# Hashed attention and a PReLU layer pair on one core: the last store's buffer and queue, the place of the maxima and the verdict, and the pair of x's first differences

## The chip, the cores and the metric

The kernel runs on one core of a Trainium2 chip. The metric is the device time of one execution in microseconds (us), the median of several runs. One more execution of the kernel was recorded by the hardware profiler; all rows below come from that recording. The engines are PE (TensorE: matmuls and transposes through the array), DVE (VectorE), ACT (ScalarE), POOL (GpSimd) and SP (SyncE, which here only issues DMAs). ACT and POOL issue DMAs too.

## What is computed

```python
# q, k, v: (4, 8, 768, 64) f32, proj: (64, 6)
q_bucket = sum over 6 bits of (q @ proj > 0) * 2**bit      # k_bucket likewise
scores = where(q_bucket == k_bucket, q @ k.T / 8, -1e9)    # per batch and head
x = softmax(scores) @ v  ->  (3072, 512)                   # heads beside each other
h = x @ w_in                                               # (3072, 2048)
g = max(h, 0) + alpha * min(h, 0)
out = g @ w_out                                            # (3072, 512) f32
```

## The kernel before, in words

There are two paths. `fast_path` computes the result; while it runs it also takes the largest magnitudes of the inputs (`largest`, lines 1079 to 1083), and `verdict` (lines 1085 to 1097) turns them into one flag. After `fast_path` PE, ACT, DVE and SP each load the flag (line 401) and branch (line 402): the general path is only entered if the flag says that the fast one wasn't safe, which is not so on these inputs. So the end of the program is, on each of these engines: its last instruction, the load of the flag, the branch over the general path, and the closing waits and barriers (lines 402 and 1284). SP's closing waits are one per DMA completion semaphore.

The fast path has two stages.

**Attention** (line 1134): 16 iterations `pi`, one for a pair of heads. PE computes scores (`sc`, line 734), ACT takes their exponentials into `pt` (line 737), DVE sums these (`accp` and `accd`, lines 745 to 759), PE multiplies with v (`av`, line 770) and adds the sums up over partitions (`sm`, line 784), and DVE divides (`divide`, line 789) in the next iteration. Beside this DVE rounds pieces of the weights (lines 587 to 644) and, in the last pairs, forms differences of x of the first batch (`sum_x`, line 842: one subtraction of 128x768 a call, read by `load_x` from DRAM, line 832).

**Products** (line 1202): 4 batches `b`. Each has 8 blocks of the first product (`f_0` to `f_7`) and 7 of the second (`z_1, z_2, z_5, z_6, z_3, z_7, z_4`), 60 blocks in all, counted by `j` in the loop. Every block is a 2x2 product done with 7 matrix products in place of 8 (steps 1, 2, 5, 6, 3, 7, 4 of `Product.step`) with sums kept in three PSUM banks a, b, c; DVE and ACT form the sums and differences around it (lines 877, 915, 919, 923, 979, 987, 1008). The engines' orders are written out by hand: each `do(...)` keeps its place in program order on its engine, so a late instruction holds all that is behind it. In the first batch alone DVE also sums up the pieces of w_out (`sum_out`, line 963).

In the before kernel `largest` runs at `j == 4` (block f_4 of batch 0) and `verdict` at the end of the same block: four small DVE instructions, a PE transpose of 128x4 (`vd`, line 1087, into bank b), and nine more on DVE.

**The end.** Blocks of z are stored as they finish. `turn_out` transposes on DVE and issues 12 stores of 32 KB on SP (line 1040). The last two parts go through `turn_last`: for the last but one, six PE transposes, two ACT copies into `o` and one store of 384 KB on ACT's queue (line 1062). For the last, PE transposes into three PSUM places `tx`, `ty`, `tz`; ACT copies `ty` into `o2`, which is stored on ACT's queue (line 1070); DVE copies `tx` (line 1068) and `tz` (line 1071) into `o`, which is stored on SP's queue (line 1072). All these `o` share the tag `o`, which has two buffers.

In the built program, every DMA that SP or ACT issues adds to one of eight completion semaphores, which are handed out in turn over both queues, in the order in which the DMAs stand in the program. A DMA's issue waits, where needed, for the one before it on the same semaphore. The 12 stores of line 1040 that belong to block z_3 and the last three stores stand in this order before the change, with the number of their semaphore: six of line 1040 (7, 0, 1, 2, 3, 4), line 1062 (5), two of line 1040 (6, 7), line 1070 (0), four of line 1040 (1, 2, 3, 4), line 1072 (5). After the change: six of line 1040 (7, 0, 1, 2, 3, 4), line 1062 (5), two of line 1040 (6, 7), line 1070 (0), one of line 1040 (1), line 1072 (2), three of line 1040 (3, 4, 5).

Of the kernel before, what the change touches and what calls it, by code (L numbers as in the profile page):

```python
# [8 lines left out]
F32 = mybir.dt.float32  # L9
# [397 lines left out]
def fast_path(  # L407
# [12 lines left out]
    nc = tc.nc  # L420
    P = 128
# [21 lines left out]
    PE, DVE, ACT, POOL = nc.tensor, nc.vector, nc.scalar, nc.gpsimd  # L443
# [117 lines left out]
    def load_weight(i):  # L561
        if i < NW:
            i = order[i]
            raw[i] = pool.tile([P, 512], moe_w_in.dtype, name=f"raw{i}", tag="raw", bufs=3)
            nc.sync.dma_start(raw[i], piece(i))
# [17 lines left out]
    def weight_clamp(i):  # L583
        if i < NW:
            i = order[i]
            x = wx[i]
            do(DVE.tensor_scalar(x, x, HI_MIN, None, op0=ALU.max, op1=ALU.max, accum_out=wmax[:, i : i + 1]))

    def weight_parts(i):
        i = order[i]  # L590
        lo, hi = halves(i)
        x = wx[i]
        wr[i] = r = pool.tile([P, 512], F32, name=f"wr{i}", tag="wr", bufs=1)
        do(DVE.tensor_scalar(
            x.bitcast(U32), x.bitcast(U32), 3, 0xC0000000, op0=ALU.logical_shift_left, op1=ALU.bitwise_xor,
        ))
        do(DVE.tensor_scalar(r.bitcast(U32), x.bitcast(U32), 0x7F800000, None, op0=ALU.bitwise_and))
        do(DVE.scalar_tensor_tensor(r, lo, 2.0 ** -52, r, op0=ALU.mult, op1=ALU.mult))
# [65 lines left out]
    def two_banks(name):  # L664
        return psum.tile([P, 2, 512], F32, name=name, tag="sc", bufs=3)
# [77 lines left out]
    def add_first(pi):  # L743
        accp[pi] = pool.tile([P, 2 * NCH, CW], F32, name=f"accp{pi}", tag="accp", bufs=1)
        do(DVE.tensor_tensor(accp[pi], p(0), p(1), op=ALU.add))  # L745
        if pi:
            nc.gpsimd.dma_start(accp[pi][:, 2:], p(2)[:, 2:], accum_op=ALU.add)
# [6 lines left out]
    def add_third(pi):  # L754
        n = 2 if pi else 4
        do(DVE.tensor_tensor(accp[pi][:, :n], accp[pi][:, :n], p(2)[:, :n], op=ALU.add))
# [66 lines left out]
    def pinned(when, ins):  # L823

        if when:
            do(ins)

    def load_x(b, *ns):
        for n in ns or range(4):
            m, kh, ch = ((0, 0, 0), (1, 1, 0), (2, 1, 1), (5, 0, 1))[n]  # L830
            t = mid.tile([P, 2, CW], F32, name=f"x{b}_{m}", tag=f"x{m}", bufs=1)
            pinned(b == 0, nc.sync.dma_start(
                t, x_s[b, 2 * kh : 2 * kh + 2].rearrange("k p s -> p k s")[:, :, ch * CW : (ch + 1) * CW],
            ))
            x_m[b, m] = t

    def sum_x(b, n, engine):

        to, a, c = ((3, 5, 0), (5, 2, 5), (4, 2, 3), (6, 4, 1))[n]
        if to != 5:  # L840
            x_m[b, to] = mid.tile([P, 2, CW], F32, name=f"x{b}_{to}", tag=f"x{to}", bufs=1)
        do(engine.tensor_tensor(x_m[b, to], x_m[b, a], x_m[b, c], op=ALU.subtract))
# [202 lines left out]
    def turn_last(n):  # L1045


        b, p, half, ch = to_turn.pop(0)
        dst = out_v[b, ch * CH : (ch + 1) * CH].rearrange("c p d -> p c d")[:, :, half * 2 * P : (half + 1) * 2 * P]

        def cells(name, at):
            ps = two_banks(f"{name}{p}")[:, 0].rearrange("p (t f) -> p t f", f=P)
            for k, (t, i) in enumerate(at):
                do(PE.transpose(ps[:, k], m2[b, p][:, i, t * P : (t + 1) * P], ident))
            return ps[:, : len(at)]

        if n == 0:
            o = late[0].tile([P, CH, P, 2], F32, name=f"o_{p}", tag="o")
            for i in range(2):
                do(ACT.copy(o[:, :, :, i], cells(f"to{i}", [(t, i) for t in range(CH)])))  # L1060

            nc.scalar.dma_start(dst, o.rearrange("p t f i -> p t (f i)"))
            return
        o = late[0].tile([P, 2, P, 2], F32, name=f"o_{p}", tag="o")
        o2 = late[0].tile([P, P, 2], F32, name=f"o2_{p}", tag="m5", bufs=1)
        ps = cells("tx", [(0, 0), (1, 0)])
        ps2 = cells("ty", [(2, 0), (2, 1)])
        do(DVE.tensor_copy(o[:, :, :, 0], ps))
        do(ACT.copy(o2.rearrange("p f i -> p i f"), ps2))
        nc.scalar.dma_start(dst[:, 2], o2.rearrange("p f i -> p (f i)"))  # L1070
        do(DVE.tensor_copy(o[:, :, :, 1], cells("tz", [(0, 1), (1, 1)])))
        nc.sync.dma_start(dst[:, :2], o.rearrange("p t f i -> p t (f i)"))


    top = const.tile([P, 4], F32, name="top")
# [58 lines left out]
    for pi in range(NPAIR):  # L1134
        i = 2 * pi

        def weight_begin():
            weight_clamp(i)
            weight_parts(i)
            add_first(pi)  # L1140

        scores(pi, [c for c in CELLS if pi or c not in ahead])
        if pi:
            divide(pi - 1, weight_begin)
        else:
            add_first(pi)
        weight_sum(i)
        weight_group(i)
        load_weight(i + 3)
        if pi == 0:  # L1150
            weight_abs(1, DVE)
        weight_clamp(i + 1)
        add_third(pi)
        add_last(pi)
        weight_parts(i + 1)
        weight_sum(i + 1)
        weight_group(i + 1)
        load_weight(i + 4)
        add_total(pi)
        weight_sums(2)  # L1160
        if pi + 1 < NPAIR:
            hash_bits(pi + 1)
        if pi + 2 < NPAIR:
            turn(pi + 2, "q")
            turn(pi + 2, "k")
        attend(pi)
        if pi + 1 == NPAIR:
            now = ff1(0, 0)
            now.step(1)
        totals(pi)  # L1170
        if pi + 1 == NPAIR:
            now.step(5)
            divide(pi)
        else:
            weight_abs(i + 2)
        if pi + 2 < NPAIR:
            load(pi + 2, "v")
        if pi in (9, 11, 15):
            load_w((9, 11, 15).index(pi))
        if pi in (9, 10, 12):  # L1180
            load_x(0, *{9: (0,), 10: (1, 3), 12: (2,)}[pi])
        if pi >= 12:
            sum_x(0, pi - 12, DVE)
        if pi == 1:
            setup_alpha()
        for name in "qk":
            magnitude(pi, name)
            if pi + 3 < NPAIR:
                load(pi + 3, name)
        if pi + 1 < NPAIR:  # L1190
            weight_abs(i + 3)


    late, psum_bc = [], []
# [7 lines left out]
    for j, (b, what, n) in enumerate(blocks):  # L1202
        n2 = n + 1 if what == "2" else 0 if n == NI - 1 else 7
        if n2 == 0:
            sides_g(b, 0)
            sum_w2(b, 0, 3, 4)
        now.step(2) if j else now.step(6)
        if j == 0:
            now.step(3)
            now.step(7)  # L1210
            now.step(2)
        now.step(22)
        if j == 4:
            largest()
        if 0 < n2 < 7:
            sides_g(b, n2)
            sum_w2(b, n2, 3, 4)
        if n2 < 7:
            sum_g2(b, n2, 3, 4)
        if j:  # L1220
            now.step(5)
            now.step(6)
            now.step(3)
            sum_w2(b, n2, 6)
            now.step(7)
            sum_w2(b, n2, 5)
            sum_g2(b, n2, 5)
        if j == 4:
            verdict()

        for n_out in [(), (0,), (1,), (2, 3), (4,), (5, 6), (7,)][j] if j < 7 else ():
            sum_out(n_out)
        for n_out in [(1,), (2, 3), (4,), (5, 6), (7,)][j] if j < 5 else ():
            load_out(n_out)
        if what == "1":
            load_w(b * NI + n + 3)

            if 0 <= n - NI + (4 if b else 2) < 2:
                load_w2(b, n - NI + (4 if b else 2))
        else:  # L1240
            load_w2(b, n + 2)
            if b + 1 < B:
                if n == 0:
                    load_x(b + 1)
                if n == 6:
                    for m in range(4):
                        sum_x(b + 1, m, DVE)
        if j + 1 < len(blocks):
            turn_out()
        else:  # L1250
            turn_last(0)
        before = now
        if j + 1 < len(blocks):
            b1, what1, n1 = blocks[j + 1]
            now = ff1(b1, n1) if what1 == "1" else ff2(b1, n1)
            now.step(1)
        before.step(4)
        if n2 < 7:
            sum_g2(b, n2, 6)
# [29 lines left out]
```

## Time and profile before

| | before |
|---|---|
| median of 5 runs | 895.84 us (895.13 to 896.10) |
| the profiled execution | 895.91 us, of which its span (first to last instruction) 894.0 us |
| busy share of the span | PE 99%, DVE 85%, ACT 46%, POOL 5% |
| mean granted TensorE clock | 0.997 |
| chain that ended last, by engine | PE 87%, DVE 7%, DMA 2%, SP's queue 2% |

The profile has these views: a page with shares and slices; the waits (which instruction waited for which engine or DMA); the chain of work that ended last; the timeline (start, duration, engine, line, operation, tiles, and in brackets the idle time of the engine just before, with what ended it; several alike are merged, with their number after an x); and all instructions of one line. A name with q behind it (SPq, ACTq) is the engine's instruction queue. Consecutive matmuls overlap: four of 128x384, or eight of 128x192, are listed with about 1.45 us, while the next group starts 1.29 or 1.30 us after them. DVE instructions overlap too, by up to 0.1 us.

### The profile page before, as it was taken

The numbers are of one execution on the slowest core, as the hardware profiler recorded it, in microseconds if no ns is written. First come the engines' busy times: TensorE is split into PE (matmuls) and PEld (weight loads), VectorE is DVE, ScalarE is ACT, GpSimd is POOL, SyncE is SP. The second block draws the span as 40 slices with busy tenths as digits, with TensorE's granted clock in tenths as the row PEclk, the third lists the DMA queues.
The fourth block names the chain that finished last, engine by engine and source line by source line (L and its number), as shares of the span: only waits on it lengthen the run. The fifth ranks groups of instructions, "written<-read, shape, count | busy, mean of one in ns | idle before, by whom it ended". The sixth has DMA issues, their size and how long they took to land.

```text
span 894.0 us, 15372 instructions
## 1 busy us (share of the span) xinstructions
PE 882.1 (99%) x5886; PEld 594.1 (66%) x5886; DVE 756.1 (85%) x1266; ACT 407.5 (46%) x726; POOL 46.2 (5%) x109
## 2 busy tenths in 40 slices
PE   9999999999999999999999999999999999999996
PEld 4544445555555445557997557997557997557996
DVE  6888988989989997899898678988668988668985
ACT  7888888888888862222112222112222112222111
POOL 1000000100100001110000000000000000000000
PEclk9999999999999999999999999999999999999998
DMA  8565586686796726578324334333435242520241
GB/s 226 143 163 136 160 237 162 174 236 198 206 282 177 231 60 218 176 288 289 132 105 134 138 124 153 137 117 108 163 103 174 101 153 83 176 95 0 95 159 57
DMA packets 124978, 140.17 MB, mean 157 GB/s; under 512 B 77776, under 2 KB 109024, under 8 KB 121312
## 3 DMA queue, kind: packets, MB, share of 16 engines
q1 hardware_dynamic: 116368, 123.90, 43.6%
q0 software_dynamic: 6384, 14.29, 6.4%
q10 hardware_dynamic: 2144, 0.92, 0.4%
q8 instruction: 48, 0.79, 0.3%
q14 instruction: 34, 0.28, 0.1%
HBM read 104.87 MB, written 28.31 MB: 149 GB/s over the span
## 4 chain that ended last, share of the span: by engine, by line
PE 87%; DVE 7%; DMA 2%; SPq 2%; issue 1%; ACT 0%; DVEq 0%; ACTq 0%
PE sc L734 15%; PE av L770 13%; PE f_0a L870 2%; PE z_3a L870 2%; PE z_6a L870 2%; PE z_5a L870 2%; PE f_2a L870 2%; PE f_1a L870 2%; PE z_2a L870 2%; PE f_3a L870 2%; PE z_7a L870 2%; PE z_1a L870 2%; PE z_4a L870 2%; PE f_7a L870 2%; PE f_6a L870 2%; PE f_5a L870 2%
## 5 line engine op out<-in xcount | busy, mean ns | idle before, releaser
L737 ACT ACTIVATE pt<-sc 128x768 f32<-128x768 f32 x192 | 154.9, 812 | 39.2 <-PE sc L734 38.7
L734 PE MATMUL sc<-qT,kT 64*128 64x384 f32 x768 | 155.1, 482 | 0.0
L770 PE MATMUL av<-pt,vn 128*32 128x385 f32 (+1 forms) x1536 | 127.4, 486 | 0.0
L770 PEld LDWEIGHTS av<-pt,vn 128*32 128x32 f32 x1536 | 48.7, 109 | 71.1 <-issue 70.1
L734 PEld LDWEIGHTS sc<-qT,kT 64*128 64x128 f32 x768 | 68.1, 187 | 39.1 <-issue 39.0
L923 DVE TENSOR_TENSOR g<-g,g 128x384 f32<-128x384 f32 x128 | 68.3, 554 | 2.2
L734 PE MATMUL sc<-qb,kb 64*128 64x384 bf16 x384 | 63.0, 323 | 0.2 <-DVE kb L719 0.2
L987 DVE TENSOR_TENSOR gs<-g,gs 128x768 f32<-128x768 f32 x56 | 53.3, 951 | 1.0
L987 DVE TENSOR_TENSOR gs<-g 128x768 f32<-128x768 f32 x56 | 53.2, 950 | 0.0
L979 DVE TENSOR_TENSOR ws<-wl 128x512 f32<-128x512 f32 x56 | 38.4, 687 | 17.1 <-DMA wl<-w_out_s 15.8
L919 DVE SCALAR_TENSOR_TENSOR g<-h,alpha 128x384 f32<-128x384 f32 x32 | 19.7, 616 | 26.1 <-ACT h L912 26.1
L734 PEld LDWEIGHTS <-kb 64*128 64x128 bf16 x384 | 19.0, 94 | 27.7 <-issue 4.3
L745 DVE TENSOR_TENSOR accp<-pt,pt 128x1536 f32<-128x1536 f32 x16 | 28.1, 1759 | 10.5 <-ACT pt L737 10.5
L712 ACT ACTIVATE qb<-hs,hb 32x384 bf16<-32x384 f32 x60 | 34.4, 574 | 1.1 <-PE hs L704 0.2
L752 DVE TENSOR_TENSOR accd<-accd,pt 128x1536 f32<-128x1536 f32 x16 | 28.1, 1759 | 1.7
L759 DVE TENSOR_TENSOR accd<-accd,accp 128x1536 f32<-128x1536 f32 x16 | 28.0, 1752 | 0.0
L751 DVE TENSOR_TENSOR accd<-pt,pt 128x1536 f32<-128x1536 f32 x16 | 28.0, 1751 | 0.0
L723 ACT ACTIVATE kb<-hs,hb 64x384 bf16<-64x384 f32 (+1 forms) x45 | 26.0, 578 | 0.6
L870 PE MATMUL f_0a<-x,wi 128*128 128x384 f32 x64 | 23.5, 489 | 0.0
L870 PE MATMUL f_5a<-x,wi 128*128 128x384 f32 x64 | 23.3, 486 | 0.0
L870 PE MATMUL f_6a<-x,wi 128*128 128x384 f32 x64 | 23.3, 486 | 0.0
L870 PE MATMUL f_7a<-x,wi 128*128 128x384 f32 x64 | 23.3, 486 | 0.0
(351 smaller groups left out, 1774.7 us busy)
## 6 DMA issues: line engine op xcount, KB each, us to landing
wi<-w_in_s SPq DMA_DIRECT2D x32, 896.0 KB, 4.7
wl<-w_out_s SPq DMA_DIRECT2D x16, 1024.0 KB, 4.8
wl<-w_out_r SPq DMA_DIRECT2D x12, 1024.0 KB, 4.8
raw<-in_moe_w_out_dram SPq DMA_DIRECT2D x16, 512.0 KB, 4.5
raw<-in_moe_w_in_dram SPq DMA_DIRECT2D x16, 512.0 KB, 4.4
w_in_s<-wsi SPq DMA_DIRECT2D x16, 448.0 KB, 5.8
vn<-in_v_dram SPq DMA_DIRECT2D x16, 384.0 KB, 4.6
x_s<-x SPq DMA_DIRECT2D x16, 384.0 KB, 4.5
```

Of the source, the lines that this page charges most:

```text
L712: do(ACT.activation(bits["q", pi][D * s : D * s + 32, cols], ps["q"][c : c + 32, 0 if engine is DVE else half, :CW], AF.Sign, bias=hb[c : ...
L734: do(PE.matmul(sc[:, s, :CW], what["k", pi][r, ks], what["q", pi][r, qs], start=first, stop=not first,))
L737: do(ACT.activation(pts[kc][:, g, :, :CW], sc[:, :, :CW], AF.Exp, scale=SCALE / DOWN))
L745: do(DVE.tensor_tensor(accp[pi], p(0), p(1), op=ALU.add))
L751: do(DVE.tensor_tensor(accd[pi], p(3), p(4), op=ALU.add))
L752: do(DVE.tensor_tensor(accd[pi], accd[pi], p(5), op=ALU.add))
L759: do(DVE.tensor_tensor(accd[pi], accd[pi], accp[pi], op=ALU.add))
L770: do(PE.matmul(av[pi][D * s + t : D * s + t + 32, g, :w], nat["v", pi][:, s, kc * D + t : kc * D + t + 32], pts[kc][:, g, s, :w], start=(k ...
L870: do(PE.matmul(self.ps[bank], self.left(left, k), self.right(right, k), start=start and k == 0, stop=k == self.nk - 1, skip_group_check=no ...
L923: do(DVE.tensor_tensor(new_g(b, to)[:, i], g_m[b, x][:, i], g_m[b, y][:, i], op=ALU.subtract))
L979: do(DVE.tensor_tensor(t, w2[b, n, x], w2[b, n, y], op=op))
L987: do(DVE.tensor_tensor(t, g2[b, n, x], g2[b, n, y], op=ALU.subtract))
```

## The change

The last `o` is taken from the tag `ws3` (two buffers of the same size, used by `sum_w2` for the blocks of z) in place of the tag `o`, and its store is issued on ACT's queue. `largest` moves from block f_4 of batch 0 to block f_1 of batch 1, and `verdict` from the end of f_4 of batch 0 to the end of f_3 of batch 1. The four differences of x for batch 0 are formed in the iterations 11, 12, 13 and 15 of the pairs, before in 12, 13, 14 and 15; for this the loads of two of x's four parts change places between iterations 10 and 12.

```diff
-        o = late[0].tile([P, 2, P, 2], F32, name=f"o_{p}", tag="o")
+
+        o = late[0].tile([P, 2, P, 2], F32, name=f"o_{p}", tag="ws3")
         o2 = late[0].tile([P, P, 2], F32, name=f"o2_{p}", tag="m5", bufs=1)
...
-        nc.sync.dma_start(dst[:, :2], o.rearrange("p t f i -> p t (f i)"))
+        nc.scalar.dma_start(dst[:, :2], o.rearrange("p t f i -> p t (f i)"))
...
         if pi in (9, 10, 12):
-            load_x(0, *{9: (0,), 10: (1, 3), 12: (2,)}[pi])
-        if pi >= 12:
-            sum_x(0, pi - 12, DVE)
+            load_x(0, *{9: (0,), 10: (2, 3), 12: (1,)}[pi])
+        if 11 <= pi < 14 or pi == 15:
+            sum_x(0, min(pi - 11, 3), DVE)
...
-        if j == 4:
+        if (b, what, n) == (1, "1", 1):
             largest()
...
-        if j == 4:
+        if (b, what, n) == (1, "1", 3):
             verdict()
```

## Prediction

> **What bounds the kernel now.** I read the page first, then the waits of PE, then the timeline where PE waited, and last the timeline of the end.
>
> ```profile
> PE 882.1 (99%) x5886; PEld 594.1 (66%) x5886; DVE 756.1 (85%) x1266; ACT 407.5 (46%) x726; POOL 46.2 (5%) x109
> ```
>
> PE is busy for 99% of the span, so an edit counts only where PE waits or after PE's last instruction. From the last pairs to batch 1 the waits of PE are three (total us, times, longest):
>
> ```profile
> PE z_2c L870 <- DVE m L1008: 0.7, 1, 0.7
> PE sm L784 <- DVE accd L759: 0.6, 1, 0.6
> ...
> PE vd L1087 <- DVE top L1083: 0.3, 1, 0.3
> ```
>
> The change touches all three neighbourhoods. PE's timeline gives what each costs with its restart, counting from the 1.29 or 1.30 us after which an undisturbed group is followed by the next:
>
> ```profile
> 381.33 1.45 PE L870 MATMUL f_4a<-x,wi 128*128 128x384 f32 x4
> 383.10 0.27 PE L1087 MATMUL vd<-ident,top 128*4 128x128 f32 x1 [0.31 <-DVE top L1083]
> 383.21 1.46 PE L870 MATMUL f_5a<-x,wi 128*128 128x384 f32 x4
> ...
> 421.99 1.46 PE L870 MATMUL z_2b<-g,wl 128*128 128x192 f32 x8
> 424.13 1.57 PE L870 MATMUL z_2c<-gs,ws 128*128 128x192 f32 x8 [0.68 <-DVE m L1008]
> ```
>
> At vd: f_5a would start at 381.33 + 1.29 = 382.62 and starts at 383.21, so vd and its wait cost 0.59, of which vd's own place is 383.21 - 383.10 = 0.11. At z_2c: due at 421.99 + 1.30 = 423.29, started at 424.13, so 0.84. From there to the end the chain of waits is PE group after group, 1.29 or 1.30 each: a gain before 424 is kept. The end:
>
> ```profile
> 879.35 5.95 SPq L1040 DMA_DIRECT2D out_dram<-o  x12
> ...
> 884.37 0.44 ACTq L1062 DMA_DIRECT2D out_dram<-o  x1
> ...
> 887.41 0.42 DVE L1068 COPY o<-tx 128x256 f32<-128x256 f32 x1 [1.98 <-DMA out_dram<-o]
> 887.75 0.42 DVE L1071 COPY o<-tz 128x256 f32<-128x256 f32 x1
> 888.20 0.40 SPq L1072 DMA_DIRECT2D out_dram<-o  x1
> ```
>
> DVE waits 1.98 for the twelve stores that read the old `o`. What follows SP's last store is in the rows of lines 402 and 1072 (durations in ns, then first and last start):
>
> ```profile
> L402 SPq EVENT_SEMAPHORE  x8: 17/17/17, 891.8 to 892.3; - x8
> ...
> L402 SPq COMPARE_BRANCH  x1: 50/50/50, 889.2 to 889.2; - x1
> ```
>
> The wait of line 1072 for its completion semaphore ended here:
>
> ```profile
> L1072 SPq EVENT_SEMAPHORE  x1: 17/17/17, 887.2 to 887.2; - x1
> ```
>
> SP ends its issue at 888.60, loads the flag (0.50), branches at 889.2 and runs again only at 891.8, 2.6 later; then its eight waits and the barrier take it to 894.0. L1072 landed 2.8 after 888.20, at 891.0: 0.8 before SP asks. So the end hangs on **when SP issues its last store**, plus 5.4, not on the landing.
>
> **The last store.** The new buffer was last read at 868.6 (z_7's step 5), so L1068 waits only for `tx` (PE until 885.26) and for DVE's own L1006 (885.08 to 885.43). It starts at about 885.4. L1071 needs `tz` (PE until 885.93): 885.98 to 886.40. ACT has issued L1070 by 886.30 (885.94 + 0.36), so the store goes out at 886.43, 1.77 earlier, as L1071 to L1072 also took 0.03; with L1072's 2.8 it lands at 889.2. Only the load of the flag is queued behind it on ACT: ACT's issue ends at 886.83, + 0.48 flag + 0.05 branch + 2.8 (its own row: branch 886.9, running again 889.7) = 890.2, before SP.
>
> But SP does not gain 1.77. The turn of the completion semaphores moves: the store takes number 2 (last used by the fourth L1040, long landed) and the **twelfth L1040** gets number 5, on which it must wait for L1062. Before, L1072 had that wait, and its row says when it ended: 887.2. So SP's last issue is now an L1040 at about 887.2, not at 884.48 as before; with the median 0.43 of that line it ends at 887.65, and SP is 888.60 - 887.65 = **0.95** earlier. Bounds: issued beside an ACT store an L1040 took 0.82 (0.39 more), and the pause after the branch was 2.6 to 3.5 on the four engines (PE's 3.5, beside two stores); that leaves 0.95 - 0.39 - 0.9, a loss of 0.34, at worst. At best SP isn't held and 1.77 is gained (ACT then ends at 890.2, SP's wait for the landing at 889.2). I take 0.95: at 887.2 ACT has finished issuing, which is nearest to the quiet rows 0.43 and 2.6. The twelfth L1040 lands 1.6 to 2.9 after its issue, by 890.1, before SP asks (891.8 - 0.95 = 890.85).
>
> The Trainium skill (DMA: Bandwidth & Descriptors, "Issuing engines are not separate DMA queues") speaks against the queue move: issuing from several engines saves the issuing sequencer's time only, usually small. The rows agree here: kept on SP, the store would still have number 5, be issued at 887.2 and end at 887.6, which is the same 0.95 from the buffer alone. By the rule read the other way, with SP freed of its last issue and held by nothing, the sum would be rival 1's. For the pause the skill (Runtime: NRT & Kernel Launch, "Instruction fetch mechanics") says that a taken branch outside the two loaded pages waits for a fetch by DMA; the rows 2.6 to 3.5 fit that, and a fetch beside stores could be the slower end.
>
> **Maxima and verdict.** On DVE the four instructions of `largest` hold back f_4u by 382.96 - 382.71 = 0.25, and the nine of `verdict` the next sum of w_out from 385.19 to 386.62 = 1.43. DVE runs without a gap from 382 to 424, but the 1.68 can't all be kept, since DVE catches up with PE in f_5: f_5p's last sum needs ACT's copy of u2, and in f_2 and f_3, where DVE waited for it, it started 2.06 after PE's step 7 (365.33 - 363.27, 374.36 - 372.30). In f_5 step 7 moves from 390.95 to 390.36 (vd's 0.59), so that sum starts at 392.42, not 393.23: a lead of 0.81. After it DVE is late again and carries 0.81 to 423.73, the sum that frees bank c. z_2c starts at 424.13 - 0.81 = 423.32, still 0.62 behind its due time 423.29 - 0.59 = 422.70. So batch 0 gains **0.81** (bounds: 0.59 if the lead is lost, 1.43 if the stall goes).
>
> In batch 1 PE pays vd's place, 0.11; its wait is gone, since the maxima are two blocks old. On DVE the verdict falls into the 1.31 that it idles before f_3's g (waiting for ACT's h, at 514.36): 512.97 + 1.43 = 514.40, covered; `largest` (0.25) falls into the 0.86 before f_1u. Bank b is read by 513.3, before f_4b at 513.65 + 0.11. If that cover were gone, f_4b would wait at most 1.43. I take a loss of **0.11**. The flag is ready at 515 instead of 387, and is read at 885.
>
> **x a pair sooner.** Nothing. In iteration 14 the old L842 stands behind the sum on which PE waits, not ahead of it:
>
> ```profile
> 316.98 1.78 DVE L759 TENSOR_TENSOR accd<-accd,accp 128x1536 f32<-128x1536 f32 x1
> 318.65 0.98 DVE L842 TENSOR_TENSOR x<-x,x 128x768 f32<-128x768 f32 x1
> 319.82 0.65 DVE L800 STREAM_TRANSPOSE st<-sm 128x192 f32<-128x192 f32 x2 [0.19 <-PE sm L784]
> ```
>
> With it gone DVE waits for sm instead. In iteration 11 it enters an idle of 1.69 (before L800 at 258.61) and takes 0.95. The swapped loads have one size; the one needed sooner was issued by 241.1 and landed within 8.6, before 256.9. Without that cover it would cost up to 0.95; PE's 0.6 at sm stays.
>
> **Sum.** -0.81 + 0.11 - 0.95 = -1.65: span 892.35, with the 1.91 outside it 894.26. The profiled 895.91 lies 0.07 above the median, so 894.2.
>
> **Rivals.** (1) *SP is not held*: the twelfth store goes out as before, and the full 1.77 counts: 893.4. The moved semaphore speaks against. (2) *z_2c's stall goes*: DVE keeps its 1.68 and PE starts at 422.70: 1.43 in place of 0.81, 893.6. ACT's 2.06 in f_2 and f_3 speaks against. (3) *The end gives it back*: SP's issue takes 0.82 and its pause 3.0: 0.79 back, 895.0. (4) *Slower*: the twelfth store, now last and beside 256 KB on ACT's queue, lands late. It decides once it lands after 890.85, 3.65 after issue; each us more costs one. Stores under load took up to 8.2 (w_out_s): 4.55 more, 898.7. The 2.9 of the same store beside 384 KB speaks against. (5) *The differences do nothing*: in the forecast.
>
> **Chances.** Forecast 0.60 (893.8 to 894.6), rival 1 0.12, rival 2 0.08, rival 3 0.14, rival 4 0.06. What a measurement can tell from no change is about 0.2%, 1.79 us: the line is 894.05. A third of the forecast's chance lies below it: faster 0.20 + 0.20 = 0.40; same 0.40 + 0.14 = 0.54; slower 0.06. The range takes in the bounds of rivals 1 to 3: 893.3 to 895.1.
>
> **What would show it.** Right: vd in batch 1 without a wait; z_2c still waits for DVE, about 0.5; L1068 without a wait on a DMA; SP's last issue an L1040 near 886.5 (887.2 - 0.70); PE's wait at sm unchanged. Wrong: SP's issue elsewhere, its pause over 3.0, or a DMA that its closing waits stop at.

## The result and the profile after

The changed kernel takes 894.45 us (median of 22 runs, 893.78 to 895.38), the kernel before, run beside it, 896.27 us (median of 42 runs). The ratio is 0.9980, with a 95% interval of 0.9974 to 0.9986: a gain of about 1.8 us. The profiled execution takes 894.38 us with a span of 892.5 us, so 1.5 less in the span than before; 894.2 and -1.65 were forecast. Single executions differ by an offset of up to 0.5 us that is already there in the first pairs of heads, where no edit acts (its cause was not separated); the profiled one of the changed kernel stands 0.06 later than that of before when PE reaches f_4. So places are compared with what stands right ahead of them, and the spans only roughly. From here on lines of the changed kernel from 1069 on are one higher than before: its copies are L1069 and L1072, its last stores L1071 and L1073.

The page's busy shares:

```profile
PE 882.7 (99%) x5886; PEld 594.8 (67%) x5886; DVE 756.0 (85%) x1266; ACT 407.1 (46%) x726; POOL 46.2 (5%) x109
```

Nothing was taken out of the work: the busy times are those of before within 0.7 us. Nor is it the clock: PE's granted clock is 1.00 up to 880 us in both profiles, and the means (0.997 before, 0.999 now) differ by what follows. The waits of PE (total us, times, longest):

```profile
PE nil L514 <- DVE hb L518: 1.2, 1, 1.2
PE sm L784 <- DVE accd L759: 0.6, 1, 0.6
PE z_2c L870 <- DVE m L1008: 0.5, 1, 0.5
PE sc L734 <- DVE kb L719: 0.2, 1, 0.2
```

`vd` is gone from the list, the wait at z_2c is shorter by 0.2, and `sm` is unchanged. PE's timeline around these places (start, us, what):

```profile
381.39 1.45 PE L870 MATMUL f_4a<-x,wi 128*128 128x384 f32 x4
382.68 1.45 PE L870 MATMUL f_5a<-x,wi 128*128 128x384 f32 x4
...
421.46 1.46 PE L870 MATMUL z_2b<-g,wl 128*128 128x192 f32 x8
423.39 1.57 PE L870 MATMUL z_2c<-gs,ws 128*128 128x192 f32 x8 [0.47 <-DVE m L1008]
...
510.32 0.27 PE L1088 MATMUL vd<-ident,top 128*4 128x128 f32 x1
510.43 1.46 PE L870 MATMUL f_4a<-x,wi 128*128 128x384 f32 x4
```

In batch 0 f_5a now follows f_4a after 1.29, with nothing between: the 0.59 of `vd` is gone. z_2c starts at 423.39, before at 424.13; with the offset of 0.06 that is 0.80 sooner. It is still late: it is due at 421.46 + 1.30 = 422.76 and comes 0.63 after. In batch 1 `vd` has no bracket, so it waits for nothing, and takes its place of 0.11. DVE's timeline of f_5 shows where part of its 1.68 went:

```profile
390.69 0.55 DVE L915 TENSOR_TENSOR f_5u<-f_5u,f_5c 128x384 f32<-128x384 f32 x1 [0.15 <-PE f_5c L870]
391.28 0.62 DVE L919 SCALAR_TENSOR_TENSOR g<-f_5u,alpha 128x384 f32<-128x384 f32 x1
392.48 0.56 DVE L915 TENSOR_TENSOR f_5p<-f_5p,f_5u 128x384 f32<-128x384 f32 x1 [0.58 <-ACT f_5u L877]
```

Before, DVE ran through f_5 without a gap. Now it waits 0.15 for PE and 0.58 for ACT (with the overlap of two DVE instructions that a wait also takes away, 0.24 and 0.66): being ahead of its old place, it has caught up with the engines that feed it, and the sum at 392.48 starts 0.75 sooner than before (393.23), 0.81 without the offset, not 1.68.

The timeline of the end:

```profile
883.74 0.40 ACTq L1062 DMA_DIRECT2D out_dram<-o  x1
...
884.72 0.42 DVE L1069 COPY o<-tx 128x256 f32<-128x256 f32 x1
...
885.34 0.42 DVE L1072 COPY o<-tz 128x256 f32<-128x256 f32 x1 [0.20 <-PE tz L1054]
885.79 0.38 ACTq L1073 DMA_DIRECT2D out_dram<-o  x1
```

The copy of `tx` has no bracket any more (1.98 of waiting before). The waits of SP at the end:

```profile
SPq L402 <- SPq L402: 2.7, 1, 2.7
SPq L1040 <- DMA out_dram<-o: 2.4, 1, 2.4
```

The rows of line 402 for SP (durations in ns, then first and last start):

```profile
L402 SPq EVENT_SEMAPHORE  x8: 17/17/17, 890.3 to 890.8; - x8
...
L402 SPq COMPARE_BRANCH  x1: 50/50/50, 887.5 to 887.5; - x1
```

And the row of the last store of line 1040, the twelfth:

```profile
L1040 SPq DMA_DIRECT2D out_dram<-o x1: 315/315/315, 886.3 to 886.3; - x1
...
DMA to landing us min/median/max: 3.3/3.3/3.3
```

SP is held 2.4 us in line 1040, and its last issue, the twelfth store, goes out at 886.3: when L1062's store has landed (883.74 + 2.6). SP runs again at 890.3, before at 891.8. Of these 1.5, PE gives 0.63 (`tz` starts at 884.86, before at 885.49) and the end about 0.9 (from `tz` to the end of the span 8.5 before, 7.6 now). The span ends 1.7 after the last of SP's eight closing waits (890.8 to 892.5); that was so before (892.3 to 894.0), and it is so in every run below, to 0.1.

### The profile page after: what moved, and what is told of

Its sections match the earlier page's. It is cut to its first block, busy times and chain, and to the rows that moved or that the text cites. A ratio compares the mean times of both kernels' runs of the same rounds, so it can differ in the third digit from the quotient of the medians.

```text
span 892.5 us, 15369 instructions
## 1 busy us (share of the span) xinstructions
PE 882.7 (99%) x5886; PEld 594.8 (67%) x5886; DVE 756.0 (85%) x1266; ACT 407.1 (46%) x726; POOL 46.2 (5%) x109
## 4 chain that ended last, share of the span: by engine, by line
PE 97%; DVE 2%; ACT 0%; issue 0%; ACTq 0%; DVEq 0%
PE sc L734 17%; PE av L770 13%; PE f_0a L870 2%; PE z_4a L870 2%; PE z_7a L870 2%; PE z_1a L870 2%; PE z_3a L870 2%; PE z_6a L870 2%; PE z_5a L870 2%; PE z_2a L870 2%; PE f_4a L870 2%; PE f_7a L870 2%; PE f_3a L870 2%; PE f_6a L870 2%; PE f_2a L870 2%; PE f_1a L870 2%
## 5 line engine op out<-in xcount | busy, mean ns | idle before, releaser
L759 DVE TENSOR_TENSOR accd<-accd,accp 128x1536 f32<-128x1536 f32 x16 | 28.0, 1751 | 0.0
L870 PE MATMUL f_2a<-x,wi 128*128 128x384 f32 x64 | 23.3, 486 | 0.0
L870 PE MATMUL f_1a<-x,wi 128*128 128x384 f32 x64 | 23.3, 486 | 0.0
L870 PE MATMUL f_4a<-x,wi 128*128 128x384 f32 x64 | 23.3, 486 | 0.0
```

Of the source, the lines that this page charges most:

```text
L759: do(DVE.tensor_tensor(accd[pi], accd[pi], accp[pi], op=ALU.add))
L870: do(PE.matmul(self.ps[bank], self.left(left, k), self.right(right, k), start=start and k == 0, stop=k == self.nk - 1, skip_group_check=no ...
```

## The experiments

The theory was that of the forecast: the gain is 0.7 to 0.8 from the maxima and the verdict, nothing from x, and about 0.95 from SP's closing, which the buffer alone would give as well. Rival Q: the move of the store to ACT's queue is what matters at the end. Rival X: x's differences matter. Four kernels each do one part of the change to the kernel before; they share 33 runs of it (median 896.47). Four more add an edit to the changed kernel, to test whether what was named as the next limit is one; they share 15 runs of before (median 896.23). Ratios are against before.

**The buffer alone.**

```diff
-        o = late[0].tile([P, 2, P, 2], F32, name=f"o_{p}", tag="o")
+        o = late[0].tile([P, 2, P, 2], F32, name=f"o_{p}", tag="ws3")
```

> The kernel before with one edit: the last o in ws3's buffer, its store still on SP. Theory (the end hangs on SP's last issue, and what follows the old buffer's wait is the semaphore that line 1062's store holds until about 887.2): DVE's copies run at about 885.4 and 886.0, but the store is still issued at about 887.2, so the span falls by 0.95 to about 893.05, as with both edits. Rival N (nothing else holds the store): it is issued at 886.43, 1.77 earlier. Rival Q (the queue is what brings the gain): no gain.

Measured: 895.15 us, ratio 0.9991 (0.9982 to 1.0000), span 893.0. The copies run without waiting (885.24 and 885.85), yet the store goes out only at 887.18. The timeline and, after it, the waits of SP:

```profile
885.85 0.43 DVE L1071 COPY o<-tz 128x256 f32<-128x256 f32 x1 [0.19 <-PE tz L1054]
887.18 0.40 SPq L1072 DMA_DIRECT2D out_dram<-o  x1
```

```profile
SPq L1072 <- DMA out_dram<-o: 2.2, 1, 2.2
```

SP had nothing else to do for 2.2 us, and for the last 0.9 of them the data is ready too (the copy ends at 886.28): the issue waits for the completion semaphore that L1062's store holds. The buffer brings SP's last issue 1.02 forward (888.20 to 887.18) and the span 1.0. In this execution `tz` starts 0.12 sooner than before (885.37), so about 0.9 belongs to the end, where 0.95 was forecast. The interval reaches 1.0000, so it is the timeline that shows the gain. Rival N falls.

**The maxima and the verdict alone.**

```diff
-        if j == 4:
+        if (b, what, n) == (1, "1", 1):
             largest()
...
-        if j == 4:
+        if (b, what, n) == (1, "1", 3):
             verdict()
```

> The kernel before with one edit: maxima and verdict in batch 1. Theory: vd's 0.59 goes, DVE's lead of 1.68 shrinks to 0.81 at f_5p, z_2c starts 0.81 earlier and still waits for DVE about 0.5, vd costs 0.11 in batch 1: span 0.70 lower, about 893.3. Rival 2 (the whole lead is kept): z_2c without a wait, span 1.32 lower. Rival (batch 1 pays it back): no change in the span.

Measured: 895.35 us, ratio 0.9994 (0.9985 to 1.0003), span 893.3, of which 0.14 is the offset at f_4 (381.19, before 381.33). The interval takes in 1, so the times alone don't settle it; PE's timeline does:

```profile
381.19 1.45 PE L870 MATMUL f_4a<-x,wi 128*128 128x384 f32 x4
382.48 1.45 PE L870 MATMUL f_5a<-x,wi 128*128 128x384 f32 x4
...
421.25 1.46 PE L870 MATMUL z_2b<-g,wl 128*128 128x192 f32 x8
423.21 1.57 PE L870 MATMUL z_2c<-gs,ws 128*128 128x192 f32 x8 [0.50 <-DVE m L1008]
```

It is that of the changed kernel: 1.29 from f_4a to f_5a, and z_2c 0.66 late. This part of the gain needs nothing of the other two.

**x's differences alone.**

```diff
-            load_x(0, *{9: (0,), 10: (1, 3), 12: (2,)}[pi])
-        if pi >= 12:
-            sum_x(0, pi - 12, DVE)
+            load_x(0, *{9: (0,), 10: (2, 3), 12: (1,)}[pi])
+        if 11 <= pi < 14 or pi == 15:
+            sum_x(0, min(pi - 11, 3), DVE)
```

> The kernel before with one edit: x's first differences in iterations 11, 12, 13 and 15. Theory: nothing, PE waits for the sum before sm in iteration 14 for 0.6 as before, span 894.0 within 0.2. Rival (the difference in iteration 14 holds up PE's sums): that wait goes, span up to 0.84 lower.

Measured: 896.43 us, ratio 1.0003 (0.9994 to 1.0012), span 893.7. The 0.3 less than before is no gain: in this execution PE stands 0.5 sooner from the first pair on. DVE's timeline at the place where the difference of iteration 14 stood:

```profile
316.51 1.75 DVE L759 TENSOR_TENSOR accd<-accd,accp 128x1536 f32<-128x1536 f32 x1
319.32 0.65 DVE L800 STREAM_TRANSPOSE st<-sm 128x192 f32<-128x192 f32 x2 [1.06 <-PE sm L784]
```

The 0.98 of the subtraction has become 1.06 of waiting for `sm`, 0.87 more than the 0.19 before, and PE's wait for L759 is still 0.6. Rival X falls.

**The queue alone.**

```diff
-        nc.sync.dma_start(dst[:, :2], o.rearrange("p t f i -> p t (f i)"))
+        nc.scalar.dma_start(dst[:, :2], o.rearrange("p t f i -> p t (f i)"))
```

> The kernel before with one edit: the last store on ACT's queue, its buffer still of the tag o. In this build too the semaphores' turn gives the twelfth L1040 number 5, so it must wait for line 1062's store; and DVE's copies into o must wait for the twelfth. Theory: the twelfth is issued at about 887.2 and lands 1.6 to 3.3 later, DVE's first copy starts at 888.9 to 890.5, the store goes out 0.8 later, ACT's flag, branch and pause of 2.8 follow: span 1.0 to 2.7 higher, about 895.2 to 896.7. Rival Q (a free SP gains): span 0.5 to 0.9 lower.

Measured: 895.27 us, ratio 0.9987 (0.9978 to 0.9996), span 892.9: 1.1 less (0.07 of it in PE, whose `tz` starts at 885.42), where the theory had 1.0 to 2.7 more. The theory took the wait of the copy L1068 to be for the twelve stores of line 1040, the last of which is held here. The timeline says otherwise:

```profile
879.44 7.82 SPq L1040 DMA_DIRECT2D out_dram<-o  x12
...
884.30 0.40 ACTq L1062 DMA_DIRECT2D out_dram<-o  x1
...
887.14 0.43 DVE L1068 COPY o<-tx 128x256 f32<-128x256 f32 x1 [1.77 <-DMA out_dram<-o]
```

The first row merges twelve issues, the last from 886.9 on (879.44 + 7.82 = 887.26 is its end); that store landed 2.5 after its start, at 889.4. L1068 ran at 887.14, so it can't have waited for it. The chain of waits names what it did wait for (start, us, what):

```profile
884.30 2.62 DMA out_dram<-o
886.92 0.03 issue
886.95 0.05 DVEq L1068
...
887.14 0.44 DVE o L1068
```

The DMA that starts at 884.30 is L1062's store. In the built program L1068 indeed waits for the count that L1062 makes on semaphore 5: the last `o` lies in the buffer that this store reads, not in one of the twelve. In the kernel before both landed at nearly the same time, L1062's store at 884.37 + 2.8 = 887.2 and the twelfth at 884.48 + 2.9 = 887.4; L1068 started at 887.41, and the view put its wait down to the later one. The rows of L1068 before fit this: the copy's last semaphore wait begins at 887.3, when the twelfth had not yet landed.

```profile
L1068 DVEq EVENT_SEMAPHORE  x4: 50/50/50, 885.1 to 887.3; - x4
```

The gain comes from SP's closing. Rows of line 402:

```profile
L402 SPq EVENT_SEMAPHORE  x8: 17/17/17, 890.5 to 891.2; - x8
...
L402 SPq COMPARE_BRANCH  x1: 50/50/50, 887.9 to 887.9; - x1
```

With the last store gone from its queue, SP's last issue is the twelfth store (886.9), held by L1062's landing as in the changed kernel. SP runs again at 890.5, before at 891.8. The last store, on ACT's queue, lands at 887.93 + 3.0 = 890.9; one of the eight waits stops there for 0.2, the last runs at 891.2, 1.1 sooner than before (892.3), and the span is 1.1 shorter. So rival Q is right that the queue alone gains at the end, and the theory wrong that it does not. But the two don't add up: with the buffer, with the queue and with both, SP's last issue goes out when L1062's store has landed (2.9, 2.6 and 2.6 after that store's start), and can't go sooner while that store holds its semaphore. Counted from `tz`, the end gains about 0.9 with the buffer, 1.1 with the queue and 0.9 with both. The queue's 0.2 more is made of small terms: SP's flag load took 0.49 (0.76 in the changed kernel) and its pause 2.6 (2.8), less the 0.2 at the landing.

**The changed kernel, with L1062's store on POOL's queue.** The order of the semaphores should then no longer hold SP.

```diff
-            nc.scalar.dma_start(dst, o.rearrange("p t f i -> p t (f i)"))
+            nc.gpsimd.dma_start(dst, o.rearrange("p t f i -> p t (f i)"))
```

> The changed kernel with line 1062's store (384 KB) on POOL's queue, so that it holds none of the eight semaphores of SP and ACT. Theory (in the changed kernel SP's last store waits for line 1062's landing; the end is the latest of SP's restart + 2.2, ACT's restart + 1.2 and the last landing + about 1.7): the twelfth L1040 goes out at about 884, SP restarts before 888 and then waits for the last store's landing (about 889.5); span 1.0 to 1.4 lower than the 892.5 of the changed kernel, about 891.2. Rival (the end hangs on the landings): no gain. Rival (a store from POOL lands late, up to 8 after issue): up to 2 longer.

Measured: 894.55 us, ratio 0.9981 (0.9971 to 0.9990), the same as the changed kernel's; span 891.9, but here PE is 0.49 sooner already at f_4 (380.90 against 381.39) and 0.46 at `tz` (884.40 against 884.86), so only about 0.2 is gained at the end, where 1.0 to 1.4 were forecast. The rows of line 402, and the last store in the timeline:

```profile
L402 SPq EVENT_SEMAPHORE  x8: 17/17/17, 887.1 to 890.2; - x8
L402 SPq COMPARE_BRANCH  x1: 50/50/50, 884.4 to 884.4; - x1
```

```profile
885.33 0.80 ACTq L1073 DMA_DIRECT2D out_dram<-o  x1
```

SP is free: it branches at 884.4, 3.1 sooner, and runs again at 887.1. But its eight waits now last until 890.2: one of them stops for 2.7, until the last store (L1073) has landed at 889.7. That store took 0.80 to issue and landed after 4.4; in the changed kernel 0.38 and 3.7. The hold of SP was real, but the landing stood close behind it, and came later than it had: with 3.7 it would have landed 0.7 sooner, which is most of the gain that was expected and is missing. Why it is slower was not separated; the 384 KB store beside it on another queue is one possible reason. Part of it is no effect of the queue: in the next two experiments, where L1062's store is on ACT's queue as in the changed kernel, the last store landed after 4.0 to 4.1.

**The changed kernel, with the sums of w_out a block sooner.** If the wait at z_2c is DVE's, work taken out of the blocks ahead of it should end it.

```diff
-        for n_out in [(), (0,), (1,), (2, 3), (4,), (5, 6), (7,)][j] if j < 7 else ():
+        for n_out in [(), (0,), (1,), (2, 3), (4, 5), (6, 7), ()][j] if j < 7 else ():
```

> The changed kernel with DVE's sums of w_out moved one block forward (pieces 4 and 5 in f_4, 6 and 7 in f_5), so that DVE has work where it caught up with PE in f_5. Theory (DVE lost 0.73 of its lead there, and z_2c's wait is what is left of its delay): DVE doesn't idle in f_5, z_2c has no wait, and the span is 0.63 to 0.74 lower than the changed kernel's, about 891.8. Rival (z_2c is held by something else): wait of 0.47 stays.

Measured: 893.49 us, ratio 0.9965 (0.9951 to 0.9978), span 891.7. PE's timeline:

```profile
421.15 1.46 PE L870 MATMUL z_2b<-g,wl 128*128 128x192 f32 x8
422.45 1.50 PE L870 MATMUL z_2c<-gs,ws 128*128 128x192 f32 x8
```

z_2c follows after 1.30 without a bracket: the 0.63 are gained. DVE's sum in f_5 no longer waits:

```profile
392.99 0.55 DVE L915 TENSOR_TENSOR f_5p<-f_5p,f_5u 128x384 f32<-128x384 f32 x1
```

The wait was DVE's backlog, and the lead that was lost in f_5 could be had by giving DVE work there. Of the 0.8 in the span 0.3 is this execution's offset (f_4 at 381.08), and the end took 0.15 longer; the interval of the runs still touches that of the changed kernel, so it is the timeline that shows the gain.

**The changed kernel, with the total of the last pair but one ahead of the weights.** In iteration 14 PE waits for L759, so L759 is put ahead of the rounding of the weights.

```diff
+        if pi == 14:
+            add_total(pi)
...
-        add_total(pi)
+        if pi != 14:
+            add_total(pi)
```

> The changed kernel with the sum of line 759 in iteration 14 alone moved ahead of the rounding of a weight piece (2.9 of DVE). Theory (PE's wait at sm stands behind DVE's chain up to line 759, not behind x's differences): the wait of 0.62 goes with its restart, span about 0.8 lower than the changed kernel's, 891.7. Rival (the wait comes back at the next pair): span unchanged.

Measured: 894.08 us, ratio 0.9969 (0.9957 to 0.9981), with the profiled execution at 894.53 and its span at 892.7, where 891.7 was forecast. PE's timeline:

```profile
318.26 0.84 PE L784 MATMUL sm<-accd,ones 128*32 128x192 f32 x16
...
419.86 1.55 PE L870 MATMUL z_1a<-gs,wl 128*128 128x192 f32 x8 [0.22 <-DVE gs L987]
...
423.49 1.57 PE L870 MATMUL z_2c<-gs,ws 128*128 128x192 f32 x8 [0.78 <-DVE m L1008]
```

The wait at `sm` is gone and PE enters the products 0.7 sooner (0.8 without the offset), but DVE, which has as much work as before, does not: PE waits at z_1a, where it did not, and longer at z_2c, which starts where it did (423.49, in the changed kernel 423.39). In this execution the gain is only moved. The timed runs lie a little lower than the profiled one, and their interval overlaps that of the changed kernel; whether some gain is left, they don't tell.

**All three edits together.**

> The changed kernel with the three edits of the runs before it in one: store on POOL, sums of w_out a block forward, the sum of line 759 first. Theory: their gains add, 1.2 + 0.7 + 0.8, span about 889.8, time about 0.9950 of the kernel before. Rival (they meet: an earlier PE leaves DVE late again at z_2c): 0.3 to 0.7 less gained.

Measured: 892.61 us, ratio 0.9956 (0.9942 to 0.9970), span 890.8, the fastest kernel of the study. The waits of PE from beginning to end:

```profile
PE nil L514 <- DVE hb L518: 1.2, 1, 1.2
PE sc L734 <- DVE kb L719: 0.2, 1, 0.2
```

With the sums of w_out sooner PE has no wait at z_1a, z_2c or `sm` any more, all in one kernel: `tz` starts at 883.63, 1.23 sooner than in the changed kernel, and the end gives the other 0.45 of the 1.7 in the span. In the pairs ahead of the edits this execution stands 0.27 later than that of the changed kernel, so PE gained 1.5: the 0.8 at `sm` and 0.6 at z_2c that were forecast do add up, and the rival (they meet at z_2c) falls. What is short of the forecast (span 890.8, not 889.8) is the end, 0.45 in place of 1.2. There too SP's waits (887.4 to 889.1) stop at the landing of the last store (884.56 + 4.1 = 888.7). Whether it beats the sums of w_out alone (0.9965) can't be told from the intervals.

## Why the prediction was right, point by point

- **`vd` and its wait in batch 0, 0.59; its place in batch 1, 0.11.** Both as measured, to 0.01. The verdict on DVE in batch 1 runs from 512.21 to 513.67, and the product behind it starts at 513.73 without a wait: covered.
- **DVE's lead, 0.81.** Measured 0.80. The sum that bounds it was forecast for 392.42 and came at 392.48, with 0.06 of offset. z_2c's lateness was forecast as 0.62 and measured as 0.63. Rival 2 (the whole 1.68 kept) falls; the sixth experiment shows what would have kept the rest.
- **x's differences, nothing.** Right, by the third experiment and by the unchanged 0.6 at `sm`.
- **The last store, 0.95.** The mechanism was right: SP's last issue is the twelfth store of line 1040, held by L1062's landing. About 0.9 was measured. Its terms were mis-sized both ways, and that they nearly cancel is luck. SP ended its issue at 886.63; the forecast, with the 0.06 of offset, was 887.65 - 0.70 + 0.06 = 887.01. That is 0.38 sooner: L1062's store landed in 2.6, not 2.8, and the issue took 0.32, not 0.43. The load of the flag then took 0.76, not 0.50, and the pause 2.77, not 2.60: 0.43 later. The last store landed in 3.7, not 2.8, which the closing hid. Rival 1 falls (SP is held 2.4). Rival 3's price (0.79) was half there, but not from its terms: the issue was not slow, of the longer pause less than half came, and the rest was the flag's load, which no rival had. Rival 4 falls by little: the twelfth store landed 3.3 after its issue, where 3.65 would have counted, at 889.65, 0.6 before SP ran again.
- **A wrong reading beside it.** "DVE waits 1.98 for the twelve stores that read the old `o`" is wrong: it waited for L1062's store, as the fourth experiment showed. The fourth experiment's own forecast, 1.0 to 2.7 longer, was wrong for this reason. The sum did not suffer, since the new buffer took away the wait whatever its cause. Nor does the span hang on SP's last issue plus 5.4 alone: it ends 1.7 after SP's last closing wait, and the landing of the last store can set that as well, as in the fourth, the fifth and the eighth experiment. That the store, kept on SP, brings "the same 0.95 from the buffer alone" was right (0.9 at the end); that the queue has nothing of its own to give was not.
- **The size of the whole.** The forecast of 894.2 stands against 894.38 profiled and 894.45 in the median. The forecast started from 895.84; beside the changed kernel the kernel before had 896.27, so its gain in the medians, 1.8, is a little over the 1.65, and in the profiled spans, 1.5, a little under. Its chances were split around a line of 0.2%, and the ratio of 0.9980 lies on that line. The Trainium skill (DMA: Bandwidth & Descriptors, "Issuing engines are not separate DMA queues") was weighed against the queue move as saving the issuing sequencer's time only. The runs show more than that: 1.1 us of span for the queue alone, where the issue itself takes 0.40, because SP's closing no longer stands behind the last store, and nothing on top of the buffer.

## What to carry to other kernels

Ask of each edit which wait it takes away, and whether another edit of the same change takes away the same one: here buffer and queue gave 0.9 and 1.1 at the end, each alone, and 0.9 together, as both run into the landing of the store before. Time saved on an engine that is behind counts only until it has caught up with its feeders; work pulled forward into that gap keeps it, and a wait removed ahead of a stretch that the other engine bounds comes back inside it. A wait of a last instruction on "a DMA" has to be followed to the semaphore and its count before a store is blamed: two that landed 0.2 us apart were mixed up here, and moving one of them apart told.

## What the runs showed of the hardware

- A DMA's issue is held by the store before it on the same completion semaphore, whichever queue that went to: SP stood 2.4 us in the changed kernel, with a store whose data had been ready since 878.5, and 2.2 with the buffer alone. With L1062's store on POOL's queue the wait was gone. Moving the last store alone to another queue moved this hold to another instruction (the fourth experiment).
- After the branch over the general path every engine paused: SP 2.6 to 3.3 us, ACT 2.6 to 3.5, DVE 2.9 to 4.3, and PE's branch is recorded with 3.4 to 4.3. Transfers of the DMA kind `instruction` run inside SP's pause (8 KB from 890.2 on before, from 888.5 on in the changed kernel); that the pause is a wait for them was not tested. The load of the flag ahead of the branch took 0.47 to 1.07: on SP 0.67 to 0.77 in the changed kernel and in the sixth and seventh experiment, 0.49 to 0.50 in the other seven. These small terms differ between runs by as much as the edits gain.
- The landing of a last store varied with what ran beside it: the 256 KB store took 2.8 to 3.1 on SP's queue and 3.0 on ACT's where L1062's 384 KB store had landed, 3.7 to 4.1 on ACT's where that store was still under way on the same queue, and 4.1 to 4.4 beside it on POOL's. The held twelfth 32 KB store took 2.5 to 3.7; the median of its line at the end is 1.6.
